# LayerNorm statistics of a fused attention and MLP kernel: ScalarE sums and GpSimd normalisation for seven tiles, earlier statistics and GpSimd normalisation for three

## The chip, the cores and the metric

The kernel runs on one core of one Trainium2 chip. The core has five engines with a queue each: TensorE (PE in the profile, PEld for its weight loads), VectorE (DVE), ScalarE (ACT), GpSimd (POOL) and SyncE (SP), which issues the DMAs here. The metric is the device time of one execution in microseconds, the median of several runs. Lower is better.

## The reference

x is 2048 tokens by 512 features. x is normalised per token; a sliding-window attention (32 heads of 16, window 256) and an MLP (512 to 1792 to 512, with a LayerNorm of its own) both work on the normalised x; the attention's output is gated by the SiLU of the MLP's and added to x.

```python
def _layernorm(x, axis=-1, eps=1e-5):
    m = jnp.mean(x, axis=axis, keepdims=True)
    v = jnp.var(x, axis=axis, keepdims=True)
    return (x - m) / jnp.sqrt(v + eps)

x = A_x
xn = _layernorm(x, axis=-1)
s = _A_ref(xn, A_wqkv, A_wo)                      # windowed attention, then @ wo
g = _silu(_B_ref(xn, B_w1, B_b1, B_w2, B_b2))     # layernorm, dense, gelu, dense
return x + s * g
```

All the change is in the first LayerNorm, which makes xn.

## The kernel before

**Tiles.** x is cut into four chunks of 512 tokens (chunk 0 to 3), each of four tiles of 128 tokens by 512 features, so 16 tiles. A tile is normalised in place and transposed by PE (four 128x128 blocks a tile, in a PSUM bank for each of four feature groups kt). Each transposed bank is split into a high part, which ACT copies to `xnT`, and a low part, which DVE computes as the difference; matmuls take the two parts in three passes.

**Order.** Every engine runs its instructions in the order of the program (class `Ordered`, lines 31 to 46); SP too from line 620 on. A preamble handles chunk 0, then the statistics of chunk 1. After it a loop over t from -16 to 128 issues work written out by hand: t below 0 is the opening stage, in which the attention's first heads are projected while x is still being normalised. The opening is in four groups of four steps. Group c (t from 4c-16) holds the query and key projection of chunk c (`job_qk(0, c)`, 12 matmuls of 512 columns), two value projections (`job_v`, 24 matmuls of 256 columns each, called v0 to v7 here) and the transposes of chunk c+1 (`job_x`, 16). From t = -12 each step also has one block of maxima (`max_block`, m = t + 12): PE writes scores into the one buffer `xy`, DVE masks them and reduces them, and the next block's scores wait for that.

**Statistics.** `layernorm` (line 81) gives for each tile two steps, `each` and `end`. `each` is `bn_stats`, `bn_aggr` and an addition of epsilon on DVE, then a power of -0.5 on POOL (`rs`). `end` is a shift (-mean times rs) of 128x1 on DVE and the normalisation by ACT as one activation with scale and bias; the last tile of chunks 0 and 1 is normalised by DVE instead. The steps of chunk 1 are issued in the preamble but for the last `end` (at t = -16); chunk 2 is at t = -13 and chunk 3 at t = -9 and t = -8, two tiles at a time (`pair`, `lns`, lines 737 to 741):

```python
lns = {-16: [ln1[3][1]], -13: pair(ln2, 0) + pair(ln2, 2), -9: pair(ln3, 0), -8: pair(ln3, 2)}
```

**POOL.** In the preamble POOL computes the low parts of the query, key and value weights (`wqb`, `wva`), and after the powers of chunk 1 it writes the ones into `vt` and makes the triangle `upper`, which the masks of `max_block` read. From then on until t = 0 it has only the powers of chunks 2 and 3.

**Banks.** The value projections and the transposes of a chunk share two PSUM banks (`ps_st`); the other transposes use `fb` and, for chunk 1, `zo`. A bank is free again when ACT (for a value projection) or ACT and DVE (for a transpose) have read it.

Of the kernel before, what the change touches and what calls it, by code (L numbers as in the profile page):

```python
# [9 lines left out]
F32 = mybir.dt.float32  # L10
F32R = mybir.dt.float32r
I32 = mybir.dt.int32
AF = mybir.ActivationFunctionType
ALU = mybir.AluOpType
# [3 lines left out]
S, D, H, DH, WIN, F = 2048, 512, 32, 16, 256, 1792  # L18
P = 128
# [5 lines left out]
EPS = 1e-5  # L25
# [24 lines left out]
def mixer_kernel(ctx, tc, x, wqk, wv, wo, w1, b1, w2, b2, out):  # L50


    nc = SimpleNamespace(**{name: Ordered(tc, name) for name in ("tensor", "vector", "scalar", "gpsimd", "sync")})

    const = ctx.enter_context(tc.tile_pool(name="const", bufs=1))
    bigp = ctx.enter_context(tc.tile_pool(name="bigp", bufs=1))
    t2 = ctx.enter_context(tc.tile_pool(name="t2", bufs=5))
    small = ctx.enter_context(tc.tile_pool(name="small", bufs=3))
# [9 lines left out]
    def split(dst_hi, dst_lo, src, eng=None):  # L68

        (eng or nc.scalar.copy)(dst_hi, src)  # L70
        nc.vector.tensor_sub(dst_lo, src, dst_hi.bitcast(F32))
# [6 lines left out]
        nc.sync.dma_start(t, src)  # L78
        return t

    def layernorm(ts, name, on_act, eager=False, n_act=4):

        n = len(ts)
        mv = small.tile([P, n, 2], F32, tag="mv", name=f"mv{name}")
        rs = small.tile([P, n], F32, tag="rs", name=f"rs{name}")
        sh = small.tile([P, n], F32, tag="shift", name=f"shift{name}")

        def each(i):  # L90

            stats(i)
            ve = small.tile([P, 1], F32, tag="ve1", name=f"ve{name}_{i}")
            nc.vector.tensor_scalar(ve, mv[:, i, 1:2], EPS, None, op0=ALU.add)
            nc.gpsimd.tensor_tensor(rs[:, i: i + 1], ve, mhalf[:, :1], op=ALU.pow)

        def shift(i):
            nc.vector.scalar_tensor_tensor(sh[:, i: i + 1], mv[:, i, 0:1], -1.0, rs[:, i: i + 1],
                                           op0=ALU.mult, op1=ALU.mult)

        def stats(i):
            st = small.tile([P, 6], F32, tag="bn", name=f"bn{name}_{i}")
            nc.vector.bn_stats(st, ts[i])
            nc.vector.bn_aggr(mv[:, i], st)

        def invert():
            ve = small.tile([P, n], F32, tag="ve", name=f"ve{name}")
            nc.vector.tensor_scalar(ve, mv[:, :, 1], EPS, None, op0=ALU.add)
            nc.gpsimd.tensor_tensor(rs, ve, mhalf[:, :n], op=ALU.pow)

        def shift_all():
            if on_act:
                nc.vector.scalar_tensor_tensor(sh, mv[:, :, 0], -1.0, rs, op0=ALU.mult, op1=ALU.mult)

        def apply(i, on_act=on_act):
            if on_act:
                nc.scalar.activation(ts[i], ts[i], AF.Identity, bias=sh[:, i: i + 1], scale=rs[:, i: i + 1])
            else:
                nc.vector.tensor_scalar(ts[i], ts[i], mv[:, i, 0:1], rs[:, i: i + 1],
                                        op0=ALU.subtract, op1=ALU.mult)  # L120

        def end(i):

            if i < n_act:
                shift(i)
            apply(i, i < n_act)
        if eager:
            return [(lambda i=i: each(i), lambda i=i: end(i)) for i in range(n)]
        return [lambda i=i: stats(i) for i in range(n)] + [invert, shift_all] + [lambda i=i: apply(i) for i in range(n)]

    def run(steps):
# [3 lines left out]
    def load_x(c, pools, name):  # L135
        return [load(*pools[i % len(pools)], x[512 * c + P * i: 512 * c + P * (i + 1), :], f"{name}_{c}_{i}")
                for i in range(4)]
# [3 lines left out]

    xs = {0: load_x(0, XE, "x")}
    big = bigp.tile([P, 2, KT, S], F32R, tag="big", name="xnT")
    x23 = bigp.tile([P, 8, 512], F32, tag="qk1", name="x_23")
    slots = []

    def open_slot(i):
# [48 lines left out]
    mhalf = const.tile([P, 4], F32, name="mhalf")  # L196
# [38 lines left out]
    def halves(dst_hi, dst_lo, src, part):  # L235

        if part != 1:
            nc.scalar.copy(dst_hi, src)
        if part != 0:
            nc.vector.tensor_sub(dst_lo, src, dst_hi.bitcast(F32))  # L240

    def split_wqk(part=None):
        n, raw = raws["qk"]
        if part != 1:
            wqs[n] = bigp.tile([P, 2, KT, P], F32R, tag=f"wb{n % 2}", name=f"wqb{n}")
        halves(wqs[n][:, 0], wqs[n][:, 1], raw, part)
# [281 lines left out]
    def open_y():  # L528

        t = bigp.tile([P, 4, 512], F32, tag="wa", name="y0")  # L530
        mlp["y"] = [t[:, i] for i in range(4)]
        for i in range(4):
            nc.sync.dma_start(mlp["y"][i], xn_d[i])
        mlp["ln"] = layernorm(mlp["y"], "C0", False)
# [91 lines left out]
    def transpose0(i):  # L626
        for kt in range(KT):
            nc.tensor.transpose(tr0[kt][:, P * i: P * (i + 1)], xs[0][i][:, P * kt: P * (kt + 1)], ident)
        for _ in range(3 if i < 3 else 0):
            nc.tensor.matmul(zo[:, 0, 0:P], ident, ident, start=True, stop=True)  # L630

    ln = layernorm(xs[0], "A0", True, True, 3)
    for i in range(4):
        ln[i][0]()
# [3 lines left out]
    ln[3][1]()  # L638
    transpose0(3)
    split_wqk(0)  # L640
    n, raw = raws["qk"]
    nc.gpsimd.tensor_tensor(wqs[0][:, 1], raw, wqs[0][:, 0].bitcast(F32), op=ALU.subtract)
    for j, raw in enumerate(raws["v"]):
        nc.vector.tensor_copy(wva[:, 0, 2 * j: 2 * j + 2], raw)
        nc.gpsimd.tensor_tensor(wva[:, 1, 2 * j: 2 * j + 2], raw, wva[:, 0, 2 * j: 2 * j + 2].bitcast(F32),
                                op=ALU.subtract)
    for kt in range(KT):
        split(big[:, 0, kt, 0:512], big[:, 1, kt, 0:512], tr0[kt])
    ln1 = layernorm(xs[1], "A1", True, True, 3)
    for i in range(4):  # L650
        ln1[i][0]()
        if i:
            ln1[i - 1][1]()
    nc.gpsimd.memset(vt[:, :, :, DH: DH + 1], 1.0)
    nc.gpsimd.affine_select(out=upper, in_=upper, pattern=[[1, P]], compare_op=ALU.is_gt,
                            fill=0.0, base=0, channel_multiplier=-1)
# [40 lines left out]
    on_pool = nc.gpsimd  # L697
# [36 lines left out]
    fills[16 * NQ, 0] = [(first_h, (0,))]  # L734
    at(16 * NQ, activate_first)

    def pair(l, a):
        return [l[a][0], l[a + 1][0], l[a][1], l[a + 1][1]]

    ln2, ln3 = (layernorm(xs[c], f"A{c}", True, True) for c in (2, 3))  # L740
    lns = {-16: [ln1[3][1]], -13: pair(ln2, 0) + pair(ln2, 2), -9: pair(ln3, 0), -8: pair(ln3, 2)}

    def fill_in(t, half):
        now[:] = t, half
# [4 lines left out]
    end = 16 * NQ  # L749
# [474 lines left out]
```

## Time and profile before

| what | value |
|---|---|
| median of three runs | 770.53 us (769.84 to 771.13) |
| the profiled execution's own time | 770.7 us |
| its span | 769.0 us |
| PE busy | 746.9 us, 97% |
| DVE busy | 533.5 us, 69% |
| ACT busy | 435.2 us, 57% |
| POOL busy | 280.4 us, 36% |

The profile is of one execution. Times in it count from the start of the span, which is 1.7 us shorter than that execution's time. An engine's busy time is a sum over its instructions; those of PE overlap and their ends are modelled, so 97% doesn't mean that PE is never held up. The granted clock is the share of full speed that PE was given. The chain of waits goes back from the last instruction to whatever released it, step by step.

The opening stage ends about 71.6 us into the span; everything the change touches lies in its part from about 10 us to 50 us.

### The profile page before, as it was taken

The page shows a single profiled execution, that of the slowest core. Times are in us where ns is not written, and L with a number is a line of the kernel's source. Part 1 is how long each engine was busy: PE and PEld are TensorE (multiplying, and loading weights), DVE is VectorE, ACT ScalarE, POOL GpSimd, SP SyncE. Part 2 cuts the span into 40 slices and gives each one's busy share as a digit, 9 for nine tenths or more (in the row PEclk, how much of TensorE's full clock was granted, in tenths as well). Part 3 has the DMA queues.
Part 4 walks back from the last instruction along what each step waited for, and adds up shares of the span by engine and source line. Part 5 has one row for each costly group of instructions (what it writes and reads, how often), then busy time and mean ns, then how long its engine had stood idle before and what let it go on. Part 6 is the DMA issues. An engine that isn't in the chain of part 4 may idle for free.

```text
span 769.0 us, 18778 instructions
## 1 busy us (share of the span) xinstructions
PE 746.9 (97%) x7428; PEld 584.1 (76%) x7428; DVE 533.5 (69%) x865; ACT 435.2 (57%) x724; POOL 280.4 (36%) x567
## 2 busy tenths in 40 slices
PE   9889999999999999999999999999999999999997
PEld 8777666666768887676676678888887888888886
DVE  7886777777777677887875447764657675576473
ACT  6536776767676675777876855444545553342001
POOL 6111666757656554665776800030101100001102
PEclk9989999999999999999999999999999999999999
DMA  7612444645446873454654274641202322243531
GB/s 260 206 44 51 108 106 124 175 114 141 99 103 180 271 225 100 103 156 125 168 156 148 62 267 140 182 160 42 83 20 78 122 73 93 83 155 123 174 96 55
DMA packets 56951, 99.40 MB, mean 129 GB/s; under 512 B 11104, under 2 KB 11360, under 8 KB 56864
## 3 DMA queue, kind: packets, MB, share of 16 engines
q1 hardware_dynamic: 56864, 98.21, 43.9%
q8 instruction: 58, 0.95, 0.5%
q14 instruction: 29, 0.24, 0.1%
HBM read 51.39 MB, written 29.62 MB: 105 GB/s over the span
## 4 chain that ended last, share of the span: by engine, by line
PE 84%; DVE 7%; ACT 4%; issue 2%; POOL 2%; DMA 1%; SPq 0%; DVEq 0%; ACTq 0%
PE acc L42 19%; PE fb L42 17%; PE zo L42 13%; PE p L42 9%; PE stb L42 8%; PE h L42 6%; PE s L42 6%; PE xy L42 5%; ACT pt L42 3%; DVE xy L42 1%; DVE mt L42 1%; PE pv L42 1%; DVE xnT L42 1%; POOL pt L42 1%; DVE bnA L42 1%
## 5 line engine op out<-in xcount | busy, mean ns | idle before, releaser
L42 POOL TENSOR_SCALAR_AFFINE_SELECT pt<-pt 128x256 f32<-128x256 f32 x480 | 193.0, 427 | 159.1 <-ACT pt L42 155.8
L42 ACT ACTIVATE pt<-stb 128x768 f32<-128x768 f32 (+1 forms) x244 | 188.7, 773 | 55.3 <-PE stb L42 46.2
L42 DVE TENSOR_REDUCE mt<-xy 128x4 f32<-128x1024 f32 (+1 forms) x128 | 152.6, 1192 | 4.4
L42 PE MATMUL acc<-w,gh 128*128 128x512 f32 x432 | 133.3, 390 | 0.0
L42 DVE COPY_PREDICATED xy<-upper,zo 128x512 f32<-128x512 int32 x112 | 77.5, 692 | 69.2 <-PE zo L42 67.3
L42 PE MATMUL fb<-xnT,wqb 64*128 64x512 f32 (+1 forms) x684 | 115.2, 405 | 0.5 <-DVE xnT L42 0.5
L42 PE MATMUL zo<-pt,vt 128*17 128x128 f32 x2880 | 103.8, 275 | 2.2 <-DVE xy L42 1.5
L42 PE MATMUL stb<-qk 64*128 64x384 f32 (+1 forms) x488 | 96.6, 392 | 7.1 <-ACT pt L42 5.7
L42 POOL TENSOR_TENSOR xo<-xo,gated 128x512 f32<-128x512 f32 x15 | 20.2, 1347 | 217.8 <-DVE gated L42 194.2
L42 PEld LDWEIGHTS zo<-pt,vt 128*17 128x17 f32 x2880 | 67.4, 97 | 39.4 <-issue 17.8
L42 PEld LDWEIGHTS acc<-w,gh 128*128 128x128 f32 x432 | 80.8, 188 | 16.5
L42 PEld LDWEIGHTS stb<-qk 64*128 64x128 f32 x488 | 45.5, 183 | 52.4 <-ACT pt L42 41.3
L42 PE MATMUL acc<-w,gl 128*128 128x512 f32 x216 | 84.2, 390 | 0.0
L42 PEld LDWEIGHTS fb<-xnT,wqb 64*128 64x128 f32 (+1 forms) x684 | 63.4, 186 | 7.4 <-DVE xnT L42 0.6
L42 PE MATMUL xy<-qk 64*128 64x256 f32 (+2 forms) x536 | 62.0, 305 | 4.9 <-DVE mt L42 4.4
L42 ACT COPY oraw<-zo 128x128 f32<-128x128 f32 x128 | 34.2, 267 | 40.4 <-PE zo L42 36.3
L42 PEld LDWEIGHTS xy<-qk 64*128 64x128 f32 x536 | 44.0, 186 | 16.7 <-DVE mt L42 9.6
L42 PEld LDWEIGHTS acc<-w,gl 128*128 128x128 f32 x216 | 40.5, 188 | 8.8 <-DVE gl L42 0.3
L42 ACT ACTIVATE gated<-acc 128x512 f32<-128x512 f32 x16 | 8.7, 596 | 65.1 <-DVE acc L42 65.1
L42 PE MATMUL s<-wos,ohl 128*128 128x512 f32 (+1 forms) x204 | 44.7, 377 | 0.0
L42 PEld LDWEIGHTS s<-wos,ohl 128*128 128x128 f32 x204 | 36.7, 188 | 7.0
L42 PE MATMUL zo<-qk 64*128 64x128 f32 x448 | 40.7, 259 | 0.0
(182 smaller groups left out, 1159.9 us busy)
## 6 DMA issues: line engine op xcount, KB each, us to landing
qk<-sh SPq DMA_DIRECT2D x128, 128.0 KB
qk<-pjr SPq DMA_DIRECT2D x64, 128.0 KB
oT_d<-oraw SPq DMA_DIRECT2D x32, 256.0 KB
w_d<-in_w_dram SPq DMA_DIRECT2D x14, 512.0 KB
x<-in_x_dram SPq DMA_DIRECT2D x16, 256.0 KB
or<-oT_d SPq DMA_DIRECT2D x16, 256.0 KB
w<-rden_d SPq DMA_DIRECT2D x16, 256.0 KB
xo<-in_x_dram SPq DMA_DIRECT2D x16, 256.0 KB
```

The costliest lines, as they stand in the source:

```text
L42: r = issue(*args, **kwargs)
```

## The change

Ten of the twelve tiles of chunks 1 to 3 get their normalisation from POOL or their statistics from ACT, or both:

- Seven tiles (two of chunk 1, the first of chunk 2, all four of chunk 3) have three steps. `total`: ACT passes the tile through Identity and accumulates the sum, and POOL makes the negative mean `nm` of it. `squares`: ACT squares the tile with `nm` as its bias and accumulates, and POOL makes variance plus epsilon and the power. `end_sums`: POOL normalises the tile.
- The other three tiles of chunk 2 keep `each` on DVE, but in the preamble, and are normalised by POOL (`on_pool`).
- The last two tiles of chunk 1 keep both steps (ACT normalises one, DVE the other); both are now in the preamble.
- All of chunk 2 is issued in the preamble, ahead of the ones in `vt` and of `upper`. Chunk 3 is issued at t = -13 (two tiles) and t = -11 (two tiles).
- ACT's passes write into a ninth tile of `x_23`, which nothing reads.

```diff
-    def layernorm(ts, name, on_act, eager=False, n_act=4):
+    def layernorm(ts, name, on_act, eager=False, n_act=4, by_sums=(), on_pool=()):
         n = len(ts)
+        nm = small.tile([P, n], F32, tag="nm", name=f"nm{name}") if by_sums else None
+        sums = small.tile([P, n, 2], F32, tag="sums", name=f"sums{name}") if by_sums else None
+
+        def total(i):
+            nc.scalar.activation(x23[:, 8], ts[i], AF.Identity, accum_out=sums[:, i, 0:1])
+            nc.gpsimd.tensor_scalar(nm[:, i: i + 1], sums[:, i, 0:1], -1.0 / D, None, op0=ALU.mult)
+
+        def squares(i):
+            nc.scalar.activation(x23[:, 8], ts[i], AF.Square, bias=nm[:, i: i + 1], accum_out=sums[:, i, 1:2])
+            ve = small.tile([P, 1], F32, tag="ve1", name=f"ve{name}_{i}")
+            nc.gpsimd.tensor_scalar(ve, sums[:, i, 1:2], 1.0 / D, EPS, op0=ALU.mult, op1=ALU.add)
+            nc.gpsimd.tensor_tensor(rs[:, i: i + 1], ve, mhalf[:, :1], op=ALU.pow)
+
+        def end_sums(i):
+            nc.gpsimd.tensor_scalar(ts[i], ts[i], nm[:, i: i + 1], rs[:, i: i + 1], op0=ALU.add, op1=ALU.mult)
 ...
         def end(i):
+            if i in on_pool:
+                nc.gpsimd.tensor_scalar(ts[i], ts[i], mv[:, i, 0:1], rs[:, i: i + 1], op0=ALU.subtract, op1=ALU.mult)
+                return
             if i < n_act:
                 shift(i)
             apply(i, i < n_act)
         if eager:
-            return [(lambda i=i: each(i), lambda i=i: end(i)) for i in range(n)]
+            return [(lambda i=i: total(i), lambda i=i: squares(i), lambda i=i: end_sums(i)) if i in by_sums else
+                    (lambda i=i: each(i), lambda i=i: end(i)) for i in range(n)]
...
-    x23 = bigp.tile([P, 8, 512], F32, tag="qk1", name="x_23")
+    x23 = bigp.tile([P, 9, 512], F32, tag="qk1", name="x_23")
...
     split_wqk(0)
+    ln1 = layernorm(xs[1], "A1", True, True, 3, by_sums=(0, 1))
+    ln2 = layernorm(xs[2], "A2", True, True, by_sums=(0,), on_pool=(1, 2, 3))
+    ln3 = layernorm(xs[3], "A3", True, True, by_sums=range(4))
+    ln1[0][0]()
     n, raw = raws["qk"]
     nc.gpsimd.tensor_tensor(wqs[0][:, 1], raw, wqs[0][:, 0].bitcast(F32), op=ALU.subtract)
...
         split(big[:, 0, kt, 0:512], big[:, 1, kt, 0:512], tr0[kt])
-    ln1 = layernorm(xs[1], "A1", True, True, 3)
+    ln1[0][1]()
+    ln1[1][0]()
+    ln1[0][2]()
+    ln1[2][0]()
+    ln1[1][1]()
+    ln1[2][1]()
+    ln1[3][0]()
+    ln1[1][2]()
+    ln1[3][1]()
+    ln2[0][0]()
+    ln2[0][1]()
+    for i in (1, 2, 3):
+        ln2[i][0]()
     for i in range(4):
-        ln1[i][0]()
-        if i:
-            ln1[i - 1][1]()
+        ln2[i][-1]()
     nc.gpsimd.memset(vt[:, :, :, DH: DH + 1], 1.0)
...
-    def pair(l, a):
-        return [l[a][0], l[a + 1][0], l[a][1], l[a + 1][1]]
-
-    ln2, ln3 = (layernorm(xs[c], f"A{c}", True, True) for c in (2, 3))
-    lns = {-16: [ln1[3][1]], -13: pair(ln2, 0) + pair(ln2, 2), -9: pair(ln3, 0), -8: pair(ln3, 2)}
+    lns = {-13: [*ln3[0], *ln3[1]], -11: [*ln3[2], *ln3[3]]}
```

## The prediction

> **What bounds the kernel now.** I read the page first, then the table of stages over the opening, the chain of waits there, the groups of POOL and ACT by form, and last the timeline of the queues that the change touches.
>
> ```profile
> PE 746.9 (97%) x7428; PEld 584.1 (76%) x7428; DVE 533.5 (69%) x865; ACT 435.2 (57%) x724; POOL 280.4 (36%) x567
> ```
>
> On average PE is the bound. In the opening stage it is not:
>
> ```profile
> core 0: us, PE busy (x) PEld busy (x) DVE busy (x) ACT busy (x) POOL busy (x), PEclk, DMA share, GB/s
> 34.00:39.00 5.00, 4.48 (x36) 3.98 (x35) 4.75 (x8) 0.59 (x1) 0.00 (x0) 1.00 0.24 53
> 39.00:44.00 5.00, 4.06 (x28) 3.15 (x26) 4.16 (x14) 2.04 (x3) 1.10 (x2) 1.00 0.00 0
> 44.00:49.00 5.00, 3.65 (x24) 2.92 (x24) 4.26 (x11) 1.87 (x3) 1.10 (x2) 0.79 0.49 111
> 49.00:54.00 5.00, 4.97 (x26) 4.23 (x26) 4.85 (x7) 2.51 (x5) 0.00 (x0) 0.53 0.24 54
> ```
>
> From 34 to 54 us DVE is nearly full, ACT and POOL mostly idle, and PE has gaps (0.52, 0.94 and 1.35 us in the first three rows); in the last two its granted clock falls to 0.79 and 0.53. The chain says which DVE work it is:
>
> ```profile
> 39.79 0.61 DVE bnA L42
> 40.43 0.19 DVE mvA L42
> 40.64 0.15 DVE veA L42
> 40.80 0.61 DVE bnA L42
> ...
> 42.62 0.10 DVE mh L42
> ...
> 45.02 0.61 DVE bnA L42
> ```
>
> A tile's statistics hold DVE for 1.01 us (39.79 to 40.80). The first two tiles of chunk 3 lie on the chain from 39.79 to 42.62, 2.8 us; the other two follow at 45.02 and cost the same: 5.7 us that the change takes off DVE. So there is something to win here; the question is what ACT and POOL, now in the chain, charge for it.
>
> **Prices.** The change puts on POOL, for a tile with three steps, two operations of 128x1 (`nm`, `ve`), a power and a normalisation of 128x512, on ACT two passes with a sum. The nearest rows:
>
> ```profile
> L42 POOL TENSOR_SCALAR_AFFINE_SELECT pt<-pt 128x256 f32<-128x256 f32 x480 | 193.0, 427 | 159.1 <-ACT pt L42 155.8 <-DMA w_d<-in_w_dram 1.2 <-DMA qk<-sh 0.9
> L42 POOL TENSOR_TENSOR pjr<-pjr,sh 128x512 fp32r<-128x512 f32 x28 | 35.8, 1280 | 0.0
> ...
> L42 POOL TENSOR_TENSOR rsA<-veA,mhalf 128x1 f32<-128x1 f32 x16 | 8.8, 551 | 29.0 <-DVE veA L42 23.5 <-DVE shiftA L42 5.5
> ...
> L42 POOL TENSOR_SCALAR_AFFINE_SELECT upper<-upper 128x128 f32<-128x128 f32 x1 | 0.6, 563 | 0.0
> L42 POOL MEMSET vt<- 128x256 f32 x1 | 0.5, 547 | 0.0
> ...
> L1212 POOL MEMSET const-bfloat16-1.0<- 128x1 bf16 x1 | 0.1, 101 | 0.0
> ```
> ```profile
> L42 ACT ACTIVATE p<-p,b1s 128x512 f32<-128x512 f32 x21 | 15.1, 720 | 2.0 <-DVE p L42 2.0
> ...
> L42 ACT CAST wqb<-wqkr 128x512 fp32r<-128x512 f32 x8 | 4.9, 616 | 0.0
> ```
>
> A power is 0.55 us, with its hand-over 0.6. A POOL normalisation lies between a one-input pass over half the elements, 0.43, and a two-input pass over all, 1.28; it has one tensor input like the select, so I take two selects less one start, 0.80. A 128x1 operation lies between a memset of 128x1, 0.10, and a power, 0.55; I take 0.20, nearer the memset, as it raises nothing to a power. ACT's pass is 0.62 without a pointer and 0.72 with one; no row shows the read-out of a sum, so between nothing and half a pass more (0.3); I take 0.18: 0.80 for `total`, 0.90 for `squares`. A hand-over between engines is about 0.06. A tile so costs POOL 0.2 + 0.2 + 0.6 + 0.8 = 1.8 us, and ACT 1.7 where its normalisation took 0.8.
>
> The length is not the main cost, the order is. `squares` cannot start before POOL's `nm` of the same tile, and POOL's `nm` stands behind the power and normalisation of the tile before. So while two tiles run, ACT waits for POOL and whatever is queued on ACT waits too.
>
> **The walk.** I wrote down each queue in the order of the changed code and let every instruction start when its engine is free and its inputs are there, with these prices and the trace's durations for the rest. The rows it is held against:
>
> ```profile
> 28.08 1.57 ACT L42 ACTIVATE x<-x,shiftA,rsA 128x512 f32<-128x512 f32 x2 [1.27 <-DVE shiftA L42]
> 29.56 0.56 ACT L42 CAST sh<-fb 128x512 fp32r<-128x512 f32 x1
> 30.02 0.59 ACT L42 COPY vt<-pv 128x512 f32<-128x512 f32 x1
> 31.38 1.07 ACT L42 CAST xnT<-tr 128x512 fp32r<-128x512 f32 x2 [0.77 <-PE tr L42]
> ```
> ```profile
> 9.96 1.50 POOL L42 TENSOR_TENSOR wqb<-wqkr,wqb 128x512 fp32r<-128x512 f32 x1 [0.87 <-ACT wqb L42]
> ...
> 18.87 0.74 DVE L42 TENSOR_SCALAR x<-x,mvA,rsA 128x512 f32<-128x512 f32 x1 [0.60 <-POOL rsA L42]
> 19.03 0.57 ACT L42 CAST sh<-xy 128x512 fp32r<-128x512 f32 x1
> ...
> 25.73 0.44 PE L42 MATMUL xy<-qk 64*128 64x128 f32 x4 [0.25 <-DMA qk<-pjr]
> ...
> 33.47 3.13 PE L42 MATMUL pv<-wva,xnT 128*128 128x256 f32 x24
> ...
> 58.12 0.51 PE L42 MATMUL xy<-qk 64*128 64x256 f32 x4
> ```
>
> The same walk over the kernel as it is puts the scores of block 8 (the last row) at 57.99, so its errors are small there; v3 (33.47) it puts at 33.97, and I give differences between the two walks where I can.
>
> *Weights.* `nm` of the first tile stands before the low part of `wqb` on POOL: ACT sums until 10.74, `nm` until 10.94, so the 1.50 us that began at 9.96 begin at 10.94. PE's second matmul needs them, `wva`'s low part follows, and v0 starts 0.75 late. PE has work until the transposes, so this much is not yet a loss.
>
> *Chunk 1.* POOL is free at 15.0 and does in order `ve`, power, `nm`, normalise (16.8), then the power of the third tile (17.4). DVE had that tile's variance at 15.1 and waits 2.3 us. The fourth tile's statistics run 17.5 to 18.7, its power ends at 19.3; the second tile is normalised by POOL at 20.1 and the fourth by DVE at 20.0. Before, chunk 1 was ready at 19.6 (18.87 + 0.74). Half a microsecond late.
>
> *ACT behind it.* The first tile of chunk 2 has its `nm` behind that normalisation, so its `squares` run 20.3 to 21.2 and `sh` (19.03 before) starts at 21.2. Its DMAs, the copies that free v0's bank and the split of chunk 1 move by about 2 us; the first scores come at 27.9 (25.73 before). That costs nothing yet: DVE used to be busy with chunk 2 then (the normalisations at 28.08 in the rows wait for its shifts) and now is not. POOL has normalised chunk 2 by 27.1 and, with the 0.55 and 0.56 of the ones and the triangle, `upper` is there at 28.1, before the first mask. If POOL were half a microsecond later at this point, the first mask would wait for it.
>
> *The step t = -13.* Chunk 3's first `total` ends on ACT at 25.7. Its `nm` must wait until POOL has done all that, 28.3. `squares` 28.3 to 29.3; `ve`, power, normalise until 30.9; second `nm` 31.1; second `squares` until 32.0. Queued behind on ACT are `sh` of chunk 1 (32.0; 29.56 before) and the copy of v2 (32.5; 30.02 before).
>
> *The step t = -11.* Two more tiles stand ahead of the copies of chunk 2's transposes: `total` 33.1 to 33.9, `squares` 34.2 to 35.1, `total` to 35.9, `nm` behind a power and a normalisation at 37.0, `squares` to 37.9. Only then do the copies start that began at 31.38: 6.3 us late in the walk. Both banks that they empty are what v3 needs, so PE stands idle but for one block of scores from 34.7 to 39.3. v3 starts 5.3 us later than before. This is the price.
>
> *Given back.* From there the two stretches of 2.8 us on DVE are gone. Not all 5.7 us come back, because PE's own work (v3 to v5, chunk 2's projection, chunk 3's transposes, six blocks of scores) then fills the stretch: 3.6 us by the walk. The scores of block 8 come at 59.7, 1.7 us late, and past that PE is the bound in both kernels, so it stays.
>
> The granted clock is the last term. In the table it falls after the stage with PE's longest gaps. Doubling PE's durations between 46.9 and 53.6 in the walk of the old kernel costs it 0.8 us; an idle stretch of four microseconds in the new one should bring the same some 8 us earlier, at a cost between 0.4 and 2.0 us by where it falls. I count 0.3 us net. The Trainium skill, TensorE: Matmul & The Clock Gate, Part 1, says that the clock halves after an idle window of about 3.4 us and returns after a busy one; the table's 0.53 agrees, and by that rule the net would be 1.2, for a sum of +2.9 instead of +2.0.
>
> Sum: 1.7 + 0.3 = +2.0 us on the profiled execution's 770.7, so 772.7. That execution lies 0.2 above the median of the runs, so 772.5 for the median. With one price moved at a time the 1.7 becomes: 128x1 operations 0.10 or 0.35: 0.6 or 3.3; normalisation 0.43 or 1.28: -0.6 or +5.8; sums for nothing or 0.2 dearer: 0.4 or 3.1. All low: -2.2; all of them high: +8.2.
>
> **Rivals.** *DVE's relief wins.* Same queues, but POOL at its floors (0.10 and 0.43) and sums nearly free: v3 is only 1.3 us late, the 3.6 us come back and the walk gives -2.2; with PE's idle stretch short enough, the half clock of the old kernel goes as well, up to -3.0. I put it at -2.5, 768.0. It decides if a tile costs POOL under about 1.55 us where I have 1.8. For it speaks that POOL and ACT are nearly empty in the table; against it that ACT must wait for POOL twice per pair of tiles whatever the passes cost.
>
> *POOL becomes the bound.* If the normalisation costs as much as a two-input pass, 1.28, six of them before `upper` make it 3 us later, the first mask waits for POOL (31.0), and v3 is 9.4 late; +5.8, 776.3. For it: no one-input 512-wide arithmetic of POOL is in the trace, and the two pointers are fetched too. Against: the select's 427 ns. The Trainium skill, GPSIMD Engine Reference, section 8, calls VectorE about twice as fast for elementwise work, which speaks against the change; doubling the 0.74 that DVE took for such a tile gives, as an estimate, 1.48 and a sum beyond this rival's, while section 4.1 of that page excepts operations of one input. No run here yet shows which holds.
>
> **How the numbers follow.** The forecast, slower by 0.6 to 4 us, gets 0.56; the relief 0.30; POOL as the bound 0.14. A run of this kernel can tell about 0.2%, 1.5 us. Of the forecast's 0.56 about 0.12 lies below that; of the relief's 0.30 about 0.06. So faster 0.24, same 0.18, slower 0.44 + 0.14 = 0.58. The range reaches down to nearly the relief's end (-2.7, 767.8) and up past POOL as the bound (+6.5, 777.0).
>
> **What would show it.** In the changed profile: POOL full from 11 to 28 us; ACT idle before the `squares` on chunk 3, released by POOL `nm`, some 2.5 us the first time; ACT's copies of chunk 2's transposes at 37 to 39 instead of 31.38; PE's gap before v3; DVE no longer full from 44 to 54; a low clock earlier. It is wrong if POOL's normalisations are 0.6 or less with `nm` under 0.15, or if `upper` is later than 29 us, or if the copies of chunk 2 are not held behind the second pair.

## The result, and the profile after

The changed kernel takes 776.73 us (median of six runs, 775.73 to 777.47), beside 770.18 us for the kernel before on the same chip (six runs, 768.61 to 771.13). The ratio is 1.0087, 95% interval 1.0072 to 1.0102: slower by 6.5 us. The profiled execution took 777.47 us with a span of 775.7. The direction was forecast, and the value lies within the range, near its end; the size was forecast at 2.0 us. The profiled execution is the longest of the six.

The engines' totals, from the page of the changed kernel:

```profile
PE 750.1 (97%) x7428; PEld 586.2 (76%) x7428; DVE 526.2 (68%) x834; ACT 437.5 (56%) x742; POOL 295.2 (38%) x591
```

DVE is relieved by 7.3 us and POOL has 14.8 us more. The table of stages over the opening (the same columns as before the change) shows what that did to PE:

```profile
24.00:29.00 5.00, 5.00 (x32) 4.16 (x32) 1.50 (x3) 0.69 (x3) 5.00 (x3) 1.00 0.95 288
29.00:34.00 5.00, 2.30 (x19) 1.72 (x17) 1.45 (x2) 1.64 (x5) 3.74 (x8) 1.00 0.76 266
34.00:39.00 5.00, 3.27 (x16) 2.94 (x18) 2.58 (x3) 3.83 (x10) 2.89 (x7) 0.52 0.50 107
39.00:44.00 5.00, 2.94 (x19) 2.75 (x16) 3.09 (x5) 3.27 (x7) 2.09 (x5) 0.50 0.25 59
44.00:49.00 5.00, 5.00 (x27) 4.57 (x27) 2.65 (x4) 0.59 (x1) 0.00 (x0) 0.62 0.00 0
49.00:54.00 5.00, 4.54 (x33) 3.59 (x33) 4.27 (x7) 0.59 (x1) 0.00 (x0) 1.00 0.02 3
```

In the first row POOL is full with three instructions and ACT does almost nothing (0.69). In the next, PE drops to 2.30 of 5 us, and then its granted clock is one half for some 13 us, from about 34.2 to 47.8. Before, it was so for about 7 us, from 46.9 to 53.6. The groups of POOL and ACT by form name the three instructions:

```profile
L42 POOL TENSOR_TENSOR rsA<-veA,mhalf 128x1 f32<-128x1 f32 x16 | 8.9, 561 | 3.3 <-DVE shiftA L42 1.5 <-DVE veA L42 1.3
L42 POOL TENSOR_SCALAR x<-x,mvA,rsA 128x512 f32<-128x512 f32 x3 | 6.2, 2094 | 0.0
...
L42 POOL TENSOR_SCALAR x<-x,nmA,rsA 128x512 f32<-128x512 f32 x7 | 5.4, 773 | 0.4
...
L42 POOL TENSOR_SCALAR nmA<-sumsA 128x1 f32<-128x1 f32 x7 | 1.8, 258 | 1.8 <-ACT x L42 1.8
L42 POOL TENSOR_SCALAR veA<-sumsA 128x1 f32<-128x1 f32 x7 | 1.3, 192 | 4.8 <-ACT x L42 4.7
```
```profile
L42 ACT ACTIVATE x<-x,nmA 128x512 f32<-128x512 f32 x7 | 5.1, 727 | 11.2 <-POOL nmA L42 11.2
L42 ACT ACTIVATE x<-x 128x512 f32<-128x512 f32 x7 | 4.4, 630 | 0.3 <-DMA x<-in_x_dram 0.2
...
L42 ACT ACTIVATION_READ_ACCUMULATOR x<-x,nmA 128x1 f32 x7 | 1.3, 192 | 0.0
```

The seven normalisations of `end_sums`, which add the negative mean, take 773 ns. The three of `on_pool`, which subtract the mean, take 2094 ns over the same 128x512 elements. ACT stands idle 11.2 us in all before its `squares`, and POOL's `nm` ends each of these waits. The longest comes before the first `squares` on chunk 3; the copies of chunk 2's transposes start behind the last:

```profile
31.05 0.72 ACT L42 ACTIVATE x<-x,nmA 128x512 f32<-128x512 f32 x1 [6.36 <-POOL nmA L42]
...
40.31 1.05 ACT L42 CAST xnT<-tr 128x512 fp32r<-128x512 f32 x2
```

The chain of waits links the two:

```profile
23.15 6.99 POOL x L42 x4
30.14 0.49 POOL vt L42
30.63 0.16 POOL upper L42
30.79 0.23 POOL nmA L42
...
40.41 0.48 ACT xnT L42
40.91 0.70 DVE xnT L42
41.66 5.49 PE pv L42 x24
```

Chunk 2's normalisations, the ones and the triangle stand on POOL ahead of chunk 3's first `nm` (30.79). The copies of chunk 2's transposes come last on ACT (40.31 in the timeline, 31.38 before), and v3 starts at 41.66 instead of 33.47. It takes 5.49 us instead of 3.13, at half clock. The scores of block 8 start at 63.85 us, 5.7 later than before:

```profile
63.85 0.50 PE L42 MATMUL xy<-qk 64*128 64x256 f32 x4
```

### The profile page after: what moved, and what is told of

It is laid out like the page before. It is cut to its first block, busy times and chain, and to the rows that moved or that the text cites. A ratio compares the mean times of both kernels' runs of the same rounds, so it can differ in the third digit from the quotient of the medians.

```text
span 775.7 us, 18801 instructions
## 1 busy us (share of the span) xinstructions
PE 750.1 (97%) x7428; PEld 586.2 (76%) x7428; DVE 526.2 (68%) x834; ACT 437.5 (56%) x742; POOL 295.2 (38%) x591
## 4 chain that ended last, share of the span: by engine, by line
PE 85%; ACT 4%; POOL 4%; DVE 4%; issue 2%; DMA 1%; DVEq 0%; ACTq 0%; POOLq 0%
PE acc L42 19%; PE fb L42 18%; PE zo L42 12%; PE p L42 9%; PE stb L42 8%; PE h L42 6%; PE s L42 6%; PE xy L42 5%; ACT pt L42 3%; PE pv L42 2%; POOL x L42 1%; POOL pt L42 1%; DVE xy L42 1%; POOL rsA L42 1%; DVE mt L42 1%
```

## The experiments

All ratios are to the kernel before, run on the same chip. Differences between two changed kernels are of medians; where the kernels ran on different chips, the kernel before itself differed by up to 1.0 us (769.76 to 770.81), and the ratios are the safer measure.

**Which kind of POOL instruction is dear.** Into the kernel before, at t = -4, ten `tensor_scalar` of 128x512 on POOL:

```diff
+        for name, a, b in forms:   # am: add, mult; sm: subtract, mult; ma: mult, add; ms: mult, subtract
+            for _ in range(2):
+                nc.gpsimd.tensor_scalar(probe, probe, ptr[name][:, 0:1], ptr[name][:, 1:2], op0=a, op1=b)
+        nc.gpsimd.tensor_scalar(probe, probe, mvp[:, 1, 0:1], mvp[:, 2, 1:2], op0=ALU.add, op1=ALU.mult)
+        nc.gpsimd.tensor_scalar(probe, probe, mvp[:, 1, 0:1], mvp[:, 2, 1:2], op0=ALU.subtract, op1=ALU.mult)
```

> The kernel before with ten more operations of POOL on a tile of their own, in the stretch where POOL is idle (t = -4): 128x512 with two pointers, add and multiply twice, subtract and multiply twice, multiply and add twice, multiply and subtract twice, then once each add-multiply and subtract-multiply with pointers of stride two as the mean has. Theory: with subtract as the first operation 2.1 us whatever the pointers, add and multiply 0.77; the two with multiply first tell whether any other form is slow. Rival (the pointer's place makes the price): subtract-multiply with plain pointers is 0.77, and both forms with pointers of stride two are 2.1.

The groups of POOL in that kernel:

```profile
L42 POOL TENSOR_SCALAR probe<-probe,p_ms 128x512 f32<-128x512 f32 x2 | 4.2, 2081 | 0.2
L42 POOL TENSOR_SCALAR probe<-probe,p_sm 128x512 f32<-128x512 f32 x2 | 4.2, 2078 | 0.2
L42 POOL TENSOR_SCALAR probe<-probe,mvp 128x512 f32<-128x512 f32 x2 | 2.9, 1428 | 0.2
L42 POOL TENSOR_SCALAR probe<-probe,p_ma 128x512 f32<-128x512 f32 x2 | 1.5, 770 | 0.2
L42 POOL TENSOR_SCALAR probe<-probe,p_am 128x512 f32<-128x512 f32 x2 | 1.5, 769 | 4.6 <-DVE p_ms L42 4.5
```

A subtraction in either place makes the instruction 2.08 us long; an addition leaves it at 0.77. The pointers' stride has no part in it: the `mvp` pair, one of each, averages 1428, near the mean of 770 and 2080. So the theory held and the rival didn't. The kernel ran once, 769.02 us.

**The addition in the kernel itself, the second pair later, and both.** For the first, DVE makes the negative mean of the three tiles; for the second, chunk 3's second pair moves behind the copies of chunk 2.

```diff
+            if i in on_pool:
+                nc.vector.tensor_scalar(nm[:, i: i + 1], mv[:, i, 0:1], -1.0, None, op0=ALU.mult)
...
-                nc.gpsimd.tensor_scalar(ts[i], ts[i], mv[:, i, 0:1], rs[:, i: i + 1], op0=ALU.subtract, op1=ALU.mult)
+                nc.gpsimd.tensor_scalar(ts[i], ts[i], nm[:, i: i + 1], rs[:, i: i + 1], op0=ALU.add, op1=ALU.mult)
```
```diff
-    lns = {-13: [*ln3[0], *ln3[1]], -11: [*ln3[2], *ln3[3]]}
+    lns = {-13: [*ln3[0], *ln3[1]], -9: [*ln3[2], *ln3[3]]}
```

> The three tiles of chunk 2 that POOL normalises by subtract and multiply (2.09 us each) take add and multiply of a negated mean instead, as the seven others do (0.77 us); DVE makes the negated mean, 0.15 us a tile. Theory (the subtraction is what is slow, it makes the triangle upper and chunk 3's first nm 3.9 us late, the rest is the order of ACT's queue and the half clock): the three take 0.75 to 0.80 us, the first mask runs at about 28.5 us instead of 30.8, and by the queue walk with the measured prices the kernel gains 2.8 to 4.0 us on the changed one, 772.7 to 774.0 us; ACT still waits for POOL before the squares of chunk 3 and the clock still falls. Rival (these three are slow because of where they stand, beside DVE's work or with pointers that DVE wrote): they stay at 2 us and the time stays within 1 us of 776.7.

> Chunk 3's second pair is issued at t = -9 instead of t = -11, behind the copies of chunk 2's transposes; nothing else. Theory (the order on ACT holds those copies back): the copies start about 3 us earlier, at 35 to 37 us instead of 40.3, v3 with them, and the kernel gains 1.7 to 3.1 us, 773.6 to 775.0 us. Rival (POOL's late triangle is all of the loss, and the queue of ACT is hidden behind it): no change within 0.7 us.

> Both edits: add of the negated mean for three tiles of chunk 2, and chunk 3's second pair at t = -9. Theory: the two prices add, v3 starts 2 us late instead of 8, DVE's relief of 5.7 us comes through, and the kernel is 1 to 3 us faster than the kernel before, 767.5 to 769.5 us. Rival (a third cost, ACT's double pass or the half clock, eats the relief): within 1 us of the kernel before or slower, 770 to 773 us.

| kernel | time, us | ratio (95%) | copies of chunk 2 | v3 starts |
|---|---|---|---|---|
| changed | 776.73 | 1.0087 (1.0072 to 1.0102) | 40.31 | 41.66 |
| addition | 774.07 | 1.0045 (1.0026 to 1.0065) | 36.75 | 38.10 |
| second pair at t = -9 | 772.71 | 1.0033 (1.0022 to 1.0044) | 35.57 | 39.39 |
| both | 768.96 | 0.9987 (0.9976 to 0.9999) | 32.41 | 35.34 |

Each edit gives back part of the loss, and with both it is gone, as expected. The addition gained 2.7 us, just short of the 2.8 expected (3.2 by the ratios). The later pair gained 4.0 us, more than the 1.7 to 3.1 expected. In its trace v3 escaped the low clock. The same stage, first with the addition alone, then with the later pair alone:

```profile
39.00:44.00 5.00, 5.00 (x26) 4.78 (x27) 3.26 (x5) 0.68 (x2) 0.00 (x0) 0.50 0.02 3
```
```profile
39.00:44.00 5.00, 5.00 (x44) 4.59 (x41) 4.44 (x8) 1.91 (x5) 0.15 (x1) 0.98 0.26 59
```

PE is full in both; at a clock of 0.98 it does 44 matmuls, at 0.50 it does 26. The same 24 matmuls of v3 take 3.14 us with the later pair and 5.49 with the addition.

**By which way the late POOL reaches the end.** The first mask waits for `upper` for 5.32 us, and `squares` wait for `nm`. Only the ones and the triangle are moved ahead of chunk 2's normalisations:

```diff
+    nc.gpsimd.memset(vt[:, :, :, DH: DH + 1], 1.0)
+    nc.gpsimd.affine_select(out=upper, ...)
     for i in range(4):
         ln2[i][-1]()
-    nc.gpsimd.memset(vt[:, :, :, DH: DH + 1], 1.0)
-    nc.gpsimd.affine_select(out=upper, ...)
```

> The changed kernel with the ones of vt and the triangle `upper` made on POOL ahead of chunk 2's four normalisations instead of behind them; nothing else moves. It asks by which of two ways the long subtractions on POOL reach the end. Theory (through ACT: the first `nm` of chunk 3 stands behind the subtractions and holds `squares`, `sh`, the copy of v2 and at last the copies of chunk 2's transposes): the first mask no longer waits and comes at 27 to 28 us instead of 30.82, but the copies still start at 39.6 to 40.4 and the time is within 1 us of 776.7. Rival (through the masks: `upper` late holds the blocks of scores and with them PE): the same early mask brings 2 to 3.5 us, 773.2 to 774.7.

It took 776.93 us, ratio 1.0085 (1.0072 to 1.0099). From its timeline:

```profile
27.14 0.75 DVE L42 COPY_PREDICATED_SCALAR xy<-upper,negc 128x512 f32 x1 [1.76 <-POOL x L42]
...
35.61 1.12 PE L42 MATMUL tr<-ident,x 128*128 128x128 f32 x4 [4.50 <-ACT vt L42]
...
40.19 1.05 ACT L42 CAST xnT<-tr 128x512 fp32r<-128x512 f32 x2
...
41.53 4.62 PE L42 MATMUL pv<-wva,xnT 128*128 128x256 f32 x24 [2.49 <-DVE xnT L42]
```

The mask comes 3.7 us earlier and nothing is won: PE's two gaps become one of 4.50 us, which ends with ACT's copy of v2, and v3 starts at 41.53, as late as in the changed kernel (41.66). The way goes through ACT.

**The clock by itself.** Spare products fill PE's gaps, to keep its clock up:

```diff
+    def spare(n):
+        for _ in range(n):
+            nc.tensor.matmul(otb, ident, ident, start=True, stop=True)
...
+            if c == 2 and k == 4:
+                spare(20)
...
+        if m == 1:
+            spare(18)
...
+        if m == 2:
+            spare(20)
```

> The changed kernel with 58 spare matmuls of 128 columns whose product nothing reads, put into three places of PE's queue where it waits in the opening stage (ahead of the second block of scores, ahead of the second transposes of chunk 2, behind the third block), so that PE keeps its full clock. Nothing else moves. Theory (the half clock from 34.4 to 47.6 us is a cost of its own, since v3 took 5.49 us in it where it takes 3.13 at the full clock): the clock stays at 1.0 over that stretch, v3 takes about 3.1 us, and the kernel gains 1.8 to 2.6 us on the changed one, 774.1 to 774.9 us. Rival (the slow clock only fills time in which PE would wait for DVE anyway): within 0.7 us of 776.7.

783.6 us, ratio 1.0172 (1.0153 to 1.0191). From PE's timeline:

```profile
30.42 4.18 PE L42 MATMUL zo<-ident 128*128 128x128 f32 x36
...
44.39 6.17 PE L42 MATMUL zo<-ident 128*128 128x128 f32 x40 [2.39 <-DVE xy L42]
50.32 1.92 PE L42 MATMUL pv<-wva,xnT 128*128 128x256 f32 x14
```

The kernel spoilt its own question: each spare product ran as two matmuls, so the groups were longer than the gaps, and the third had to wait for DVE's mask and pushed v3 to 50.32.
Again with seven products in the first two gaps only:

> The changed kernel with spare products of two 128x128 tiles (result unread) where PE stands idle: seven ahead of the second block of scores and seven ahead of the second half of chunk 2's transposes. By the earlier probe one such product takes 0.23 us, so each group takes 1.6 us of gaps that are 2.15 and 2.28 us long, and delays nothing. Theory (the half clock that follows PE's gaps is a term of the loss, about 2 us): the granted clock stays above 0.9 from 34 to 44 us, v3 takes 3.1 to 3.6 us instead of 5.49, and the time is 774.1 to 775.1. Rival (the low clock only fills what PE would have waited for anyway): the clock rises in the same way, v3 is shorter, and the time stays within 0.7 us of the changed kernel's 776.7.

776.9 us, ratio 1.0091 (1.0076 to 1.0105). The stages and v3 of this kernel:

```profile
34.00:39.00 5.00, 3.60 (x33) 3.03 (x31) 2.58 (x3) 3.93 (x10) 2.76 (x9) 1.00 0.43 94
39.00:44.00 5.00, 1.97 (x12) 1.97 (x13) 2.71 (x5) 3.27 (x7) 2.47 (x5) 0.89 0.31 70
44.00:49.00 5.00, 4.85 (x28) 4.04 (x27) 3.85 (x5) 0.59 (x1) 0.00 (x0) 0.77 0.00 2
```
```profile
42.03 4.63 PE L42 MATMUL pv<-wva,xnT 128*128 128x256 f32 x24 [3.08 <-DVE xnT L42]
```

The clock stayed up until about 43 us, and the time is the same, as the rival said: v3 starts no earlier (42.03 us, in an execution that is already 0.4 us later at v2 than the one profiled for the changed kernel, 27.46 and 27.08). PE simply waits longer, 3.08 us before v3, for the low parts that DVE makes behind ACT's copies. But after that wait the clock was low over v3 again (4.63 us), so this run does not price the part that lies over v3. That part is 2.36 us in the changed kernel's trace (5.49 less 3.13), and no run removed it alone.

Pairs of traces indicate that it reaches the end. With `upper` ahead, v3 starts at 41.53 and takes 0.87 us less than in the changed kernel, and block 8 comes 1.34 us earlier (62.51). With the later pair, v3 starts 1.29 us after that of the addition alone and takes 2.35 less, and block 8 comes 1.34 us earlier (58.89 and 60.23). Each trace is one execution, though, and how long the clock is low differs from one to the next: of the six executions of the changed kernel, the profiled one has the lowest mean granted clock, 0.991, and the longest time, 777.47 us; the one with the highest, 0.996, took 775.73.

**The order within a pair.** The addition, the later pair, and both `total`s of a pair ahead of its `squares`:

```diff
+    def pair(l, a):
+        return [l[a + j][k] for k in range(3) for j in range(2)]
+
+    lns = {-13: pair(ln3, 0), -9: pair(ln3, 2)}
```

> Add for chunk 2's three tiles, chunk 3's second pair at t = -9, and in each pair of chunk 3 both totals ahead of both squares, so that the second tile's nm no longer stands behind the first one's power and normalisation. Theory (ACT's wait for POOL inside a pair, 1.28 us each, is a price of the order): the wait is under 0.3 us, and the kernel gains 0.8 to 1.5 us on the version without that order (768.96), 767.5 to 768.2 us. Rival (that wait is hidden behind PE): within 0.4 us of 769.0.

767.89 us, as the theory said; ratio 0.9971 (0.9962 to 0.9980): faster than the kernel before. The wait inside a pair is gone. ACT waits for chunk 3's `nm` only once, 1.74 us ahead of the first pair, the copies are back at 31.84, and the clock is 1.00 in every stage from 24 to 59 us.

**Each part of the change alone.** Chunk 3 alone by sums (second pair at t = -8, chunks 1 and 2 as before), and chunks 1 and 2 alone as changed (with the addition, chunk 3 as before). The lines that differ:

```diff
+    ln1 = layernorm(xs[1], "A1", True, True, 3)
+    ln2 = layernorm(xs[2], "A2", True, True)
+    ln3 = layernorm(xs[3], "A3", True, True, by_sums=range(4))
+    lns = {-16: [ln1[3][1]], -13: pair(ln2, 0) + pair(ln2, 2), -9: pair(ln3, 0), -8: pair(ln3, 2)}
```
```diff
+    ln3 = layernorm(xs[3], "A3", True, True)
+    lns = {-9: pair(ln3, 0), -8: pair(ln3, 2)}
```

> One part alone: chunks 1 and 2 as in the kernel before, chunk 3's four tiles by ACT's sums and POOL, totals ahead, at t = -9 and t = -8 where their statistics stood before. Theory (DVE's 5.7 us on the chain are worth some 3 us once nothing else waits): 1.5 to 3.5 us faster than the kernel before, 767.3 to 769.3 us, and the half clock of the kernel before (46.9 to 53.6 us) is gone or shorter. Rival (the double pass on ACT holds back sh and the transposes' copies as much as DVE's statistics did): within 1 us of the kernel before.

> The other part alone: the preamble as changed, with add for chunk 2's three tiles, and chunk 3 as in the kernel before (statistics on DVE at t = -9 and t = -8). Theory (the preamble's part moves work off DVE that the late first scores then don't use): between 1 us faster and 1 us slower than the kernel before, 769.8 to 771.8 us. Rival (chunk 2's statistics, 5.7 us on DVE before the first mask, are worth as much as chunk 3's): 2 us faster or more, under 769 us.

Chunk 3 alone took 770.19 us, ratio 1.0008 (0.9999 to 1.0017); chunks 1 and 2 alone 771.28, ratio 1.0022 (1.0011 to 1.0033). Neither half gains: for chunk 3 the rival was right, and chunks 1 and 2 come out a little slower. Both carry the 1.3 us of the next experiment (the matmuls of the last section take 393 ns in both traces), which have nothing to do with the opening; without them, as an estimate, chunk 3 alone would be slightly faster than the kernel before and chunks 1 and 2 alone about the same. In the first, the second pair comes too late for the transposes, as its timeline says:

```profile
47.03 0.33 PE L42 MATMUL tr<-ident,x 128*128 128x128 f32 x1 [1.67 <-POOL x L42]
47.78 0.76 PE L42 MATMUL tr<-ident,x 128*128 128x128 f32 x5 [0.43 <-POOL x L42]
```

In the second, DVE's chain over chunk 3 is still there. Together, as in the kernel above, they gain more than the two halves do. There chunk 3 also stands earlier (t = -13 and -9 instead of -9 and -8). That POOL must be done with chunk 2 early for chunk 3 to run early is how I read it, and no run varies that alone.

**A loss far from the change.** Behind block 8 PE is the bound, yet the span is longer by 6.7 us where block 8 is late by 5.7. The groups of the last section, in the kernel before and in the changed one:

```profile
L42 PE MATMUL acc<-w,gh 128*128 128x512 f32 x432 | 133.3, 390 | 0.0
```
```profile
L42 PE MATMUL acc<-w,gh 128*128 128x512 f32 x432 | 134.6, 393 | 0.0
```

Three nanoseconds on 432 matmuls are 1.3 us, and every kernel above with the new tiles `nm` and `sums` shows the 393; the kernel before with the ten POOL operations shows 390. These tiles were taken from `small`, a pool that lies ahead of the MLP's `gh`. The edit takes them from a pool of their own among the attention's:

```diff
+    stp = attn.enter_context(tc.tile_pool(name="stp", bufs=3))
...
-        nm = small.tile([P, n], F32, tag="nm", name=f"nm{name}") if by_sums else None
-        sums = small.tile([P, n, 2], F32, tag="sums", name=f"sums{name}") if by_sums else None
+        nm = stp.tile([P, n], F32, tag="nm", name=f"nm{name}") if by_sums else None
+        sums = stp.tile([P, n, 2], F32, tag="sums", name=f"sums{name}") if by_sums else None
```

> The changed kernel with its two new small tiles (`nm` and `sums`) taken from a pool of their own among the attention's pools, instead of from the pool `small` that lies ahead of the MLP's pools; the order of all instructions stays. It asks where the 1 us behind the scores of block 8 comes from. In the last section three matmuls of `project` (two with `gh`, one with `gl` as weights) take 0.680 us in the kernel before and in the kernel before with the probe, and 0.686 in every kernel that allocates `nm` and `sums`; over 216 such threes that is 1.3 us. Theory (the two tiles push the MLP's tiles to other addresses, and PE is slower there): the three take 0.680 us again, the mean of the `gh` matmuls falls from 393 to 390 ns, and the time is 775.0 to 775.9. Rival (the addresses have nothing to do with it): 393 ns and 776.2 to 777.3.

> The fastest kernel so far (addition instead of subtraction, chunk 3's second pair at t = -9, both `total`s of a pair ahead of its `squares`; 767.89) with the same move of `nm` and `sums`. Theory: 390 ns in the last section and 766.2 to 767.1, faster than the kernel before by 0.4% or more. Rival: 767.5 to 768.3.

The group is back at 390 ns in both. From the second:

```profile
L42 PE MATMUL acc<-w,gh 128*128 128x512 f32 x432 | 133.3, 390 | 0.0
```

The changed kernel took 776.12 us with it (774.54 to 777.97, ratio 1.0073, 1.0057 to 1.0089), between the two expectations: its runs spread over 3.4 us, too wide for a difference of 1.3, and in its trace the stretch from block 8 to the end is as long as in the changed kernel's (711.7 and 711.9 us). The fastest kernel went from 767.89 to 766.62 us, ratio 0.9954 (0.9940 to 0.9969), as the theory said; the interval overlaps that of 0.9971, but in the traces the stretch behind block 8 falls from 712.0 to 710.9 us, where the kernel before has 710.9 too. That the two tiles' place costs the 3 ns is shown; which property of the address does it is not.

## Why the prediction was right or wrong

**Right: the direction, its mechanism and its place.** The order of the queues costs more than the passes. ACT waits for POOL's `nm`, chunk 3's second pair stands ahead of the copies of chunk 2's transposes, v3 waits for these. Moving only that pair gained 4.0 us. The first wait on chunk 3 was 6.36 us where some 2.5 were expected, for the reason below. The small prices held: `nm` 258 and `ve` 192 ns (0.20 forecast), power 561, the normalisation with an addition 773 (0.80), and the read-out of a sum 0.19 (0.18), an instruction of its own.

**Right: weights and chunk 1 cost nothing that lasts.** Chunk 1 was ready at 19.4 us, even before the old 19.6 where 20.1 was forecast, `sh` started at 20.26 (21.2 forecast) and the first scores at 26.71 (27.9).

**Wrong: one price for all POOL normalisations.** This is the step that failed. Ten at 0.80 were assumed; three took 2.09, which puts 3 x 1.29 = 3.9 us on POOL ahead of `upper` and of chunk 3's first `nm`. `upper` was done at 30.8 instead of 28.1, and what follows is late by nearly the same amount: the first `squares` at 31.05 (28.3 forecast), `sh` at 34.62 (32.0), the copies at 40.31 (37.9). The prediction named this as its breaking point ("`upper` later than 29 us"). 2.09 lies beyond the upper end, 1.28, that the prediction had set. `end_sums` and `on_pool` were taken for the same instruction though the diff shows that one adds and the other subtracts, and no row of POOL had either form. The addition alone gained 2.7 us of the 4.5 us by which the forecast was short.

Term by term, on the profiled executions: v3 starts 8.19 us later (5.3 forecast) and takes 2.36 longer; block 8 is only 5.73 late, so 4.82 are given back (3.6 forecast, and the 0.8 that the walk puts on the old low clock); behind block 8 it is 1.0 more (nothing forecast). That makes 6.7, the difference of the spans. The range held because its upper end lay past the dearest rival.

The Trainium skill, GPSIMD Engine Reference, section 4.1, has operations of one input run on GpSimd at roughly the line rate. The 773 ns are near that: DVE normalised two such tiles in the changed kernel, in 0.55 and in 1.01 us. The 2094 ns are not.

**The rival "POOL becomes the bound"** gave 776.3, close to what was measured, but the closeness is luck and only half of it held. Its cause was another (three tiles at 2.09, not all at 1.28), and the way it named, the first mask, is not the one that costs: with an early mask the time stayed at 776.93.

**Wrong: the clock at 0.3 us.** The low clock moved earlier, as forecast, but lasted 13 us instead of about 7, and lay over v3. PE's idle time came in three gaps (2.15, 2.28 and 2.06 us), not in one stretch of four. The earlier part of the low clock only fills time in which PE would wait (776.9 us with the clock kept up there). Over v3 it is 2.36 us in the profiled execution, and the pairs of traces above indicate that it reaches block 8; what it is worth in the median of the runs, whose mean granted clocks are higher, stays open.

**Missing: the last section.** The prediction took for granted that what is late at block 8 "stays". To the 5.7 us, 1.3 come from the place of two small tiles by the matmuls' times; together 7.0, where the span shows 6.7.

**The rival "DVE's relief wins"** was right about what is there to win, though not in this order: with the addition, the later pair and its order within, the gain over the kernel before is 0.29%, and with the tiles in a pool of their own 0.46%, 4.1 us by the medians on one chip (766.62 and 770.69), more than the 2.5 that the rival had.

## What to carry to other kernels

When an engine takes over a step, price each form of instruction by a row of exactly that form, and where there is none, expect that two forms that compute the same may differ by a factor; here it was add against subtract. Work that is moved to an idle engine belongs behind whatever the bound engine is waiting for in that queue: with the same instructions, chunk 3's second pair made the kernel 0.45% slower ahead of a copy and 0.13% faster behind it. When a span grows by more than the last changed stage explains, compare the mean times of groups that the change never touched; new tiles in a shared pool move its neighbours.

## What was not expected of the hardware

- On POOL, a `tensor_scalar` over 128x512 takes 0.77 us with add and mult in either order and 2.08 with a subtract in either place.
- 128x512 matmuls with `gh` as weights run at 393 or 390 ns by where 144 bytes a partition of small tiles (three buffers each of 4 and of 8 floats) are placed.
- A 128x128 product of f32 tiles ran as two matmuls (18 products, 36 records, 4.18 us).
- The granted clock does not follow the gaps of one schedule alone. With chunk 3 alone by sums and with chunks 1 and 2 alone, PE is equally busy from 44 to 49 us (2.91 of 5 us in both); in the five microseconds after, the clock is 0.66 in the first:

```profile
49.00:54.00 5.00, 5.00 (x34) 4.72 (x33) 4.24 (x7) 1.40 (x3) 0.00 (x0) 0.66 0.01 3
```

and 1.00 in the second:

```profile
49.00:54.00 5.00, 4.37 (x39) 3.73 (x41) 4.93 (x7) 2.56 (x5) 0.00 (x0) 1.00 0.23 52
```

- It changes on a grid of 3.41 us. Every low stretch in the opening of the 14 traces lasts 3.41, 6.83 or 13.65 us, one, two or four times 3.41. The traces from 10 to 76 us can be cut into pieces of that length that end where the clock changes. It fell behind each of the 11 full-clock pieces in which PE was busy for 0.55 of the time or less (0.55 in the kernel before, 0.32 in the changed one), and behind none with 0.65 or more. The grid lies differently against the start from one execution to the next. With chunk 3 alone a piece from 45.8 to 49.2 us has 0.51, and the clock falls; with chunks 1 and 2 alone the pieces from 41.5 to 51.7 have 0.67, 0.77 and 0.69, and it doesn't. Its return follows no such border: it came behind low pieces of 0.80 and 0.89 in two kernels, and not behind 0.81 and 0.92 in two others.

The Trainium skill, TensorE: Matmul & The Clock Gate, Part 1, has the clock halved after an idle window of about 3.4 us that runs free of the kernel's start. The length and the free start agree with these pieces. By these traces the window need not be idle throughout, nor one gap be that long: in the changed kernel the clock fell behind a gap of 2.15 us and the beginning of one of 2.28, and in the kernel before none from 33 to 47 us was longer than 1.54.
